# First batch set tile by tile, batch 1's loads one group earlier on GpSimd, eight empty steps ahead of the fourth piece of z

## Chip, cores and metric

One core of a Trainium2 chip runs the whole program. The metric is the time of one execution on the device in microseconds (us); lower is better. A profiled execution also has a span, from its first to its last instruction, and every time of a stretch or an instruction below is read from that one.

## What is computed

Eight batches of packed attention, then two feed-forward layers over all 4608 tokens:

```
p_packed = sm_attn(p, k, v)                  # 32 packed queries a head, 8 heads, 576 keys of 64
out      = sm_attn(q, p_packed, p_packed)    # 576 queries against the 32 packed rows
x  = out.transpose(0, 2, 1, 3).reshape(4608, 512)
h  = x @ moe_w_in ; x  = (h - tanh(h)) @ moe_w_out            # 512 -> 2048 -> 512
h  = x @ moe2_w_in; g  = s * relu(h)**2 + b ; out = g @ moe2_w_out
```

All weights arrive as 64-bit floats, and the kernel converts them to 32-bit floats itself, bit by bit. Products are made as three passes of 32-bit reduced floats: a matrix is split into a high and a low part, and high x low, high x high and low x high are summed.

## The kernel before

**Two stages.** Until about 800 us the kernel does attention and the first layer, batch by batch, and on the side turns the second layer's weights into a form kept in device memory. After that the class `SecondMLP` does the second layer. The change touches only the first stage.

**Tiles.** A batch has two halves of 288 tokens (hf 0 and 1), and a half has 16 tiles j of 128 hidden columns. Attention's last product is folded into the first layer: for each batch, `make_z` forms z (the packed values times `w_in`) in four pieces c of 512 columns, each used by four tiles, and `second_stage` forms the attention weights a of a half. For each tile, `mm1` (L464) multiplies z by a in six passes, an activation step forms h - tanh(h) and splits it into gh and gl, and `mm2` (L504), two tiles later in batch 0 and three later after that, multiplies by `w_out` in twelve passes.

**Three ways for the activation step.** "v" is `act1` and `split_g`: ScalarE makes tanh, VectorE subtracts (L473), ScalarE makes gh, VectorE makes gl (L135). "b" and "p" are `act_bank`: in "b" VectorE subtracts tanh in the bank of h (L481); in "p" TensorE subtracts it, with a 32-bit product by the matrix `minus` (L484). In both, ScalarE makes gh, TensorE subtracts gh from the bank (L487), and ScalarE copies the rest as gl. `HOW` gives the way of each tile of batch 0; later batches use "v" throughout.

**Batch 0 in four parts.** Its 32 tiles run as four parts of eight: tiles 0 to 7 of half 0, then of half 1, then tiles 8 to 15 of half 0, then of half 1. Meanwhile the first layer's weights are converted: `w1_steps(c, i)` is half a piece of `w_in`, `wo1_steps(j)` is 128 rows of `w_out`. One such conversion is a step on ScalarE (L119) and four on VectorE (L121, L123, L126, L129); a `wo1_steps` then splits, with ScalarE for the high part (L138) and VectorE or GpSimd for the low part (L140).

**Who sets the order.** Nothing is planned by cost. Each of these jobs is a generator, and each `yield` ends one step. `first_weights` runs groups of conversions, of z and of half 1's attention weights through `in_turn`, which goes round the members of a group and lets the next group make one step early. `attention` runs `first_weights`, then, for each batch b, z pieces 2 and 3 of b, half 1's weights of b, and `step_p`, two times `stage1`, z pieces 0 and 1 and half 0's weights of b+1. A `wait(n)` in it is n empty steps. The tile loop calls `slot()` six times a tile (once in mm1, once after the activation step, four times in mm2), and each call makes steps of `attention` (`fill`) and, on every third, of the second layer's conversion (`more`). In batch 0 until `w_out` is converted, part n makes `AFTER[n]` steps at once behind mm1 and spreads `SLOTS[n]` over six slots; after that each tile makes `CATCH_UP` steps at once and one in each slot. `until(key, fill)` makes steps at once until a thing that the next product needs has been issued.

**Queues.** SP issues most loads. GpSimd's queue issues batch 1's and later batches' k, v and q (`load_k`, `load_v`, `load_q`: L170, L177, L178, L240) and, in the kernel before, also runs ten of the low-part subtractions. Each engine works its queue in order.

Of the kernel before, what the change touches and what calls it, by code (L numbers as in the profile page):

```python
# [13 lines left out]
ALU = mybir.AluOpType  # L14
# [4 lines left out]
def pack_attention_two_mlps(ctx, tc, q, k, v, p, w_in1, w_out1, w_in2, w_out2, s_in, b_in, out):  # L19
# [33 lines left out]
    LAND = 14  # L53
    W_K, W_P, W_PK, W_PV, W_E, W_Q = 5, 1, 5, 1, 7, 5

    AFTER, SLOTS = (6, 5, 4, 1), (5, 3, 4, 1)
    HOW = "p" * 8, "b" * 8, "v" * 8, "v" * 8
    AHEAD, CATCH_UP, FIRST_W = 13, 4, (23, 24, 25, 26, 27, 40, 41, 42, 43, 44)
    EXP_LO, EXP_HI = 2.0 ** -15, 2.0 ** 16 * 1.875
    assert 2 * R == P and NB == 2 * C and 4 * M == P and 2 * D == P and H * D == DM  # L60

# [89 lines left out]
    def split_wo(j, tag, eng, x):  # L151
        t = wopool.tile([P, 2, DM], F32R, tag=f"wo{j}", name=f"{tag}_{j}")
        wo[j] = (t[:, 0], t[:, 1])
        yield from split_seq(t[:, 0], t[:, 1], x, eng)
# [294 lines left out]
    def wait(n):  # L449
        for _ in range(n):  # L450
            yield
# [80 lines left out]
    def both(gens):  # L532
        gens = list(gens)
        while gens:
            for g in list(gens):
                try:
                    next(g)
                except StopIteration:
                    gens.remove(g)
                    continue  # L540
                yield
# [14 lines left out]
    with tc.manual_schedule():  # L556
# [51 lines left out]
        def wo1_steps(j):  # L608
            while j == NF - 1 and ("wo", 13) not in done:
                yield  # L610
            src = stg["wo", j]
            x = words(src)[0].bitcast(F32)
            yield from to_f32(x, src, wopool.tile([P, 2, DM], I32, tag=f"wo{j}", name=f"t_{j}")[:, 0])
            yield from split_wo(j, "wo1", nc.gpsimd if 1 < j < 12 else nc.vector, x)
            done.add(("wo", j))
            if j in (5, 7):
                load_wo1(j + 3, j + 4)
            if j == 11:
                load_wo1(13)
            if j == NF - 1:  # L620
                free()
# [16 lines left out]

        def in_turn(*groups):

            groups = [[call_late(g) for g in group] for group in groups]
            for n, group in enumerate(groups):
                for i, _ in enumerate(both(group)):
                    yield
                    if i == min(AHEAD, 4 * len(group)) and n + 1 < len(groups):
                        for g in groups[n + 1]:
                            next(g)

        def call_late(f):
            g, *a = f  # L650
            yield from g(*a)

        def until(key, gen):
            forced.append(key)
# [16 lines left out]
        take_turn()  # L671
        load_wo1(0, 1, 2, 3, 4, 5, 6, 7)
        make_identity(nc, ident)
        nc.scalar.mul(minus, ident, -1.0)
        nc.vector.memset(ones, 1.0)

        run(step_p(0))
# [13 lines left out]
        def first_weights():  # L691
            yield from in_turn(
                [(w1_steps, 1, 0)], [(w1_steps, 1, 1)],
                [(wo1_steps, 0), (wo1_steps, 1)],
                [(first_z, 1), (wo1_steps, 2), (wo1_steps, 3)],
                [(wo1_steps, 4), (wo1_steps, 5)],
                [(second_stage, 0, 1), (wo1_steps, 6), (wo1_steps, 7)],
                [(w1_steps, 2, 0)], [(w1_steps, 2, 1)],
                [(wo1_steps, 8), (wo1_steps, 9)],
                [(first_z, 2), (wo1_steps, 10), (wo1_steps, 11)],  # L700
                [(w1_steps, 3, 0)], [(w1_steps, 3, 1)],
                [(wo1_steps, 12), (wo1_steps, 13), (second_loads,)],
                [(first_z, 3), (wo1_steps, 14), (wo1_steps, 15)])

        pend = []

# [66 lines left out]
        def make_zs(b, c):  # L773
            while (b - 1, 1, c) not in mm1_done:
                yield
            yield from make_z(b, c)
            done.add(("z", b, c))

        def attention():

            yield from first_weights()
            for b in range(B):
                if b:
                    for c in range(2, NCH):
                        yield from make_zs(b, c)
                    yield from second_stage(b, 1)
                if b + 1 == B:
                    return
                if b:
                    load_q(b + 1, 0)  # L790
                if b + 2 < B:
                    load_p(b + 2)
                nxt = (b + 2, 0) if b + 2 < B else None
                yield from step_p(b + 1)
                yield from stage1(b + 1, 0, (b + 1, 1), (b + 1, 1))
                yield from stage1(b + 1, 1, nxt, nxt)
                if b:
                    for c in range(2):
                        yield from make_zs(b + 1, c)
                    yield from second_stage(b + 1, 0)  # L800
                else:
                    yield from both([seq(make_zs(1, 0), make_zs(1, 1)), second_stage(1, 0)])
                load_q(b + 1, 1)
# [4 lines left out]
        def slot():  # L808
            ticks[0] += 1
            if owed[0]:  # L810
                owed[0] -= 1
                next(fill, None)
            if ("wo", NF - 1) not in done:
                n = SLOTS[part[0]]
                for _ in range(ticks[0] * n // 6 - (ticks[0] - 1) * n // 6):
                    next(fill)
                return
            if ticks[0] % 3 == 1:
                next(more, None)
            next(fill, None)  # L820

        owed = [0]

        def owe():
# [4 lines left out]
        for b in range(B):  # L829
            if b:  # L830
                parts = [(hf, range(NF)) for hf in range(2)]
            else:
                parts = [(hf, js) for js in (range(NF // 2), range(NF // 2, NF)) for hf in range(2)]
            for hf, js in parts:
                part[0] += 1
                last = (b == B - 1 and hf == 1)
                if last:
                    until(("a", b, hf), fill)
                    run(fill)
                    run(more)  # L840
                    att.close()
                    second = SecondMLP(tc, ctx, wslot, w2_d, wo2_d, x2t, g2_d, s_sb, bias, out)
                    fill = second.early(lambda c: (B - 1, 1, c) in mm1_done)
                acc = new_acc(f"{b}_{hf}_{js[0]}")
                for j in js:
                    c = j // CH
                    until(("z", b, c), fill)
                    until(("a", b, hf), fill)
                    h = mm1(b, hf, j, slot)
                    if ("wo", NF - 1) not in done:  # L850
                        for _ in range(AFTER[part[0]]):
                            next(fill)
                    elif ("a", 1, 0) not in done:
                        for _ in range(CATCH_UP):
                            next(fill)
                    if j % CH == CH - 1:
                        mm1_done.add((b, hf, c))
                    how = HOW[part[0]][j - js[0]] if b == 0 else "v"
                    on_pe = how != "v"
                    t = act_bank(h, f"{b}_{hf}_{j}", how == "p") if on_pe else act1(h, f"{b}_{hf}_{j}")  # L860
                    if on_pe:
                        next(t)
                    between = None
                    if pend and len(pend[-1]) == 5:
                        a_, j_, js_, t_, st_ = pend.pop()
                        if hasattr(t_, "send"):
                            def between(t_=t_, at=(a_, j_, js_), st_=st_):
                                pend.append((*at, next(t_), st_, True))
                        else:
                            pend.append((a_, j_, js_, split_g(t_, f"1_{b}_{hf}_{j}", nc.vector), st_, True))  # L870
                    slot()
                    if len(pend) + (between is not None) >= LAG[b > 0]:
                        a_, j_, js_, g_, st_, _ = pend.pop(0)
                        until(("wo", j_), fill)
                        mm2(a_, j_, js_, g_, owe if st_ and b else slot, between)
                        if st_:
                            store_x2(*st_, a_)
                            if b == 0 and st_[0] == 0 and js[0]:
                                load_part(0, hf)
                    elif between:  # L880
                        between()
                    if on_pe:
                        next(t)
                    pend.append((acc, j, js, t, (b, hf) if j == js[-1] else None))
# [451 lines left out]
```

## Time and profile before

| | us |
|---|---|
| median of 3 runs | 1511.85 (1509.85 to 1512.5) |
| profiled execution, its own time | 1508.74 |
| its span | 1507.0 |
| batch 0: part 0, from its first mm1 | 36.06 to 74.87 |
| part 1 | 74.87 to 111.54 |
| part 2 | 111.54 to 138.54 |
| part 3 | 138.54 to 171.25 |

A part begins where the first mm1 of its first tile begins. The span holds 1460.0 us of matmul records on TensorE (97%), 1070.7 on VectorE (71%), 753.1 on ScalarE (50%) and 333.0 on GpSimd (22%). Matmuls overlap and their ends are modelled, so a full TensorE row does not mean that it ran at its peak; what a stretch is worth is seen from the starts of its products and from the waits between them.

### The profile page before, as it was taken

How to read it: one execution, taken by the hardware profiler on the slowest of the kernel's cores; microseconds unless marked ns; L12 is line 12 of the kernel's file. 1: busy time of each engine (PE TensorE's matmuls, PEld its weight loads, DVE VectorE, ACT ScalarE, POOL GpSimd, SP SyncE). 2: the span in 40 equal slices, each digit the busy share in tenths (PEclk: the TensorE clock that was granted, in tenths of full speed). 3: DMA queues.
4: the chain of work that ended last, by engine and by line, in shares of the span. 5: the costliest groups of instructions: out<-in, count | busy, mean ns of one | idle time of the engine just before them, and what ended most of it. 6: DMA issues, size and time to landing. Idle time of an engine off the chain costs nothing. (4 is left out here: it accounts for less than half of the span.)

```text
span 1507.0 us, 28083 instructions
## 1 busy us (share of the span) xinstructions
PE 1460.0 (97%) x10512; PEld 1376.0 (91%) x10512; DVE 1070.7 (71%) x2074; ACT 753.1 (50%) x1459; POOL 333.0 (22%) x542
## 2 busy tenths in 40 slices
PE   6779899999999999999999999999999999999998
PEld 4668798998989899898999999999999999999998
DVE  4886878879787787876555767767777766565554
ACT  4554344444444444443344656656666655454443
POOL 0249452643446353523001000000021000000000
PEclk6899999999999999999999999999999999999999
DMA  9446455544535344433328456465487987676683
GB/s 275 168 138 166 109 143 136 153 140 121 153 102 150 104 130 117 119 79 129 114 100 309 188 226 257 171 238 224 186 312 279 309 267 191 216 243 197 219 246 84
DMA packets 252185, 271.62 MB, mean 180 GB/s; under 512 B 112784, under 2 KB 191888, under 8 KB 252048
## 3 DMA queue, kind: packets, MB, share of 16 engines
q1 hardware_dynamic: 225952, 222.68, 45.2%
q0 software_dynamic: 22368, 46.17, 11.5%
q8 instruction: 82, 1.34, 0.4%
q10 hardware_dynamic: 3728, 0.98, 0.3%
q14 instruction: 55, 0.45, 0.1%
HBM read 161.61 MB, written 108.13 MB: 179 GB/s over the span
## 5 line engine op out<-in xcount | busy, mean ns | idle before, releaser
L504 PE MATMUL acc<-gh,wo 128*128 128x288 f32 x2040 | 418.5, 296 | 0.2 <-DVE wo L140 0.2
L504 PEld LDWEIGHTS acc<-gh,wo 128*128 128x128 f32 x2040 | 329.8, 189 | 0.5 <-DVE wo L140 0.4
L504 PE MATMUL acc<-gl,wo 128*128 128x288 f32 x1020 | 309.8, 304 | 5.7 <-ACT wo L138 2.8
L472 ACT ACTIVATE t<-h 128x288 f32<-128x288 f32 x240 | 98.5, 411 | 297.9 <-PE h L464 261.9
L504 PEld LDWEIGHTS acc<-gl,wo 128*128 128x128 f32 x1020 | 192.3, 189 | 34.4 <-issue 20.0
L464 PE MATMUL h<-a2h,z 128*128 128x288 f32 x1024 | 214.0, 297 | 1.5 <-ACT z L445 1.5
L473 DVE TENSOR_TENSOR t<-h,t 128x288 f32<-128x288 f32 x240 | 107.7, 449 | 140.5 <-ACT t L472 139.3
L942 DVE TENSOR_TENSOR x<-B,x 128x768 fp32r<-128x768 f32 x158 | 147.2, 950 | 73.7 <-ACT x L1199 59.6
L240 POOL DMA_DIRECT2D q<-in_q_dram x224 | 135.2, 611 | 227.6 <-DVE qT L374 184.0
L464 PEld LDWEIGHTS h<-a2h,z 128*128 128x128 f32 x1024 | 165.0, 189 | 2.2 <-ACT z L445 1.7
L464 PE MATMUL h<-a2l,z 128*128 128x288 f32 x512 | 157.6, 308 | 8.3 <-ACT gl L488 6.3
L1043 PE MATMUL Y<-x,w 128*128 128x384 f32 x864 | 158.5, 336 | 0.0
L1269 PE MATMUL Y<-x,w 128*128 128x384 f32 x864 | 153.4, 335 | 0.2 <-DVE u L942 0.2
L170 POOL DMA_DIRECT2D k<-in_k_dram x224 | 136.4, 616 | 69.2 <-DVE kT L290 60.8
L1043 PEld LDWEIGHTS Y<-x,w 128*128 128x128 f32 x864 | 151.3, 188 | 0.0
L1269 PEld LDWEIGHTS Y<-x,w 128*128 128x128 f32 x864 | 150.2, 188 | 0.8 <-ACT x L1199 0.5
L464 PEld LDWEIGHTS h<-a2l,z 128*128 128x128 f32 x512 | 97.2, 190 | 25.3 <-ACT gl L488 9.3
L1199 ACT CAST x<-B 128x768 fp32r<-128x768 f32 x116 | 93.7, 833 | 40.7 <-DMA B<-g 26.4
L1043 PE MATMUL X<-x,w 128*128 128x384 f32 x576 | 108.0, 336 | 0.0
L1043 PE MATMUL Z<-x,w 128*128 128x384 f32 x576 | 107.9, 336 | 0.0
L135 DVE TENSOR_TENSOR gl<-t,gh 128x288 fp32r<-128x288 f32 x239 | 106.8, 447 | 0.0
L1269 PE MATMUL X<-x,w 128*128 128x384 f32 x576 | 103.0, 336 | 1.3 <-DVE w L942 1.3
(181 smaller groups left out, 2208.7 us busy)
## 6 DMA issues: line engine op xcount, KB each, us to landing
g<-g SPq DMA_DIRECT2D x190, 384.0 KB, 3.1
B<-g SPq DMA_DIRECT2D x116, 384.0 KB, 4.5
w<-w_d POOLq DMA_DIRECT2D x28, 512.0 KB, 6.5
B<-x2t SPq DMA_DIRECT2D x24, 384.0 KB, 5.3
g<-s SPq DMA_DIRECT2D x23, 384.0 KB, 2.7
out_dram<-g SPq DMA_DIRECT2D x184, 48.0 KB, 1.8
x2t<-xs SPq DMA_DIRECT2D x15, 576.0 KB, 3.6
w1s<-in_moe_w_in_dram SPq DMA_DIRECT2D x16, 512.0 KB, 8.0
```

What stands on the lines that cost most here:

```text
L135: (eng or nc.vector).tensor_tensor(out=lo, in0=x, in1=hi.bitcast(F32), op=ALU.subtract)
L170: nc.gpsimd.dma_start(out=t[p0:p0 + 32, e], in_=rows[a][:, e, :, u * 32:u * 32 + 32])
L240: nc.gpsimd.dma_start(out=t[p0:p0 + 32], in_=src.rearrange("(n r) d -> r n d", r=32))
L464: nc.tensor.matmul(h[:, :HB], zt[:, zi, g, f0:f0 + P], a[:, g], start=(n == 0), stop=(n == 3 * G - 1))
L472: nc.scalar.activation(t, h[:, :HB], AF.Tanh)
L473: nc.vector.tensor_tensor(out=t, in0=h[:, :HB], in1=t, op=ALU.subtract)
L504: nc.tensor.matmul(acc[m][:, :HB], w[:, m * P:(m + 1) * P], x, start=(j == js[0] and i == 0), stop=(j == js[-1] and i == 2))
L942: self.nc.vector.tensor_tensor(out=o, in0=a, in1=b, op=op)
L1043: self.nc.tensor.matmul(bank[:, f, :self.TH], w[:, f, a, kt], x[:, b, kt], start=(p in ("P1", "P5", "P6") and m == 0), stop=(m == 5), skip ...
L1199: self.nc.scalar.copy(self.xs[(7 * self.NBK + n) % self.XS][:, 0], self.ready[0])
L1269: nc.tensor.matmul(bank[:, ft, :T], w[:, kk, u, ft], x[:, v, kk], start=first and p in ("P1", "P5", "P6"), stop=last, skip_group_check=True)
```

## The change

- Batch 0's steps are set tile by tile: `STEPS` has a number for each of its 32 tiles, spread over that tile's slots; the steps made at once (`AFTER`, `CATCH_UP`) are gone. `HOW` is set tile by tile too: 17 "p", 13 "b" and 2 "v" where there were 8, 8 and 16. `FIRST` holds the same four parts in the same order.
- The low parts of rows 2 to 10 of `w_out` are subtracted by VectorE; GpSimd keeps row 11 alone.
- `in_turn` starts the next group earlier (behind two or three steps of a group instead of up to thirteen), and only its conversions.
- `second_loads` (batch 1's p by SP, and 34 loads of k, v and q by GpSimd) moves from the group of rows 12 and 13 to the group of the first half of `w_in`'s piece 3; z piece 3 goes with rows 12 and 13.
- `minus` is made by VectorE's memset and a GpSimd subtraction instead of ScalarE. The steps of attention behind which the first piece of `w_in` is converted (`FIRST_W`) are others.
- In every later batch eight empty steps come ahead of z piece 3.

```diff
-    AFTER, SLOTS = (6, 5, 4, 1), (5, 3, 4, 1)
-    HOW = "p" * 8, "b" * 8, "v" * 8, "v" * 8
-    AHEAD, CATCH_UP, FIRST_W = 13, 4, (23, 24, 25, 26, 27, 40, 41, 42, 43, 44)
+    STEPS = 8, 13, 14, 11, 14, 10, 12, 15, 0, 6, 9, 13, 9, 5, 0, 3, 5, 5, 11, 9, 6, 12, 8, 11, 18, 14, 15, 13, 12, 13, 10, 7
+    HOW = "ppbbpppppppvvbbppbppppbbbbbpbbbp"
+    FIRST = (0, 0, 8), (1, 0, 8), (0, 8, 16), (1, 8, 16)
+    FIRST_W = 11, 16, 18, 26, 28, 29, 31, 40, 43, 44
...
-            yield from split_wo(j, "wo1", nc.gpsimd if 1 < j < 12 else nc.vector, x)
+            yield from split_wo(j, "wo1", nc.gpsimd if j == 11 else nc.vector, x)
...
-            groups = [[call_late(g) for g in group] for group in groups]
+            groups = [[(f, f(*a)) for f, *a in group] for group in groups]
             for n, group in enumerate(groups):
-                for i, _ in enumerate(both(group)):
+                for i, _ in enumerate(both([g for _, g in group])):
                     yield
-                    if i == min(AHEAD, 4 * len(group)) and n + 1 < len(groups):
-                        for g in groups[n + 1]:
-                            next(g)
+                    if i == len(group) and n + 1 < len(groups):
+                        for f, g in groups[n + 1]:
+                            if f in (w1_steps, wo1_steps):
+                                next(g)
...
-        nc.scalar.mul(minus, ident, -1.0)
+        nc.vector.memset(csum, 0.0)
+        nc.gpsimd.tensor_tensor(out=minus, in0=csum[:, 0], in1=ident, op=ALU.subtract)
...
-                [(w1_steps, 3, 0)], [(w1_steps, 3, 1)],
-                [(wo1_steps, 12), (wo1_steps, 13), (second_loads,)],
-                [(first_z, 3), (wo1_steps, 14), (wo1_steps, 15)])
+                [(w1_steps, 3, 0), (second_loads,)], [(w1_steps, 3, 1)],
+                [(first_z, 3), (wo1_steps, 12), (wo1_steps, 13)],
+                [(wo1_steps, 14), (wo1_steps, 15)])
...
                     for c in range(2, NCH):
+                        yield from wait(8 * (c == 3))
                         yield from make_zs(b, c)
...
-            if ("wo", NF - 1) not in done:
-                n = SLOTS[part[0]]
-                for _ in range(ticks[0] * n // 6 - (ticks[0] - 1) * n // 6):
+            if ("wo", NF - 1) in done and ticks[0] % 3 == 1:
+                next(more, None)
+            if ("a", 1, 0) in done or tile[0] >= len(STEPS):
+                next(fill, None)
+                return
+            n = STEPS[tile[0]]
+            for _ in range(ticks[0] * n // 6 - (ticks[0] - 1) * n // 6):
+                if ("a", 1, 0) not in done:
                     next(fill)
-                return
-            if ticks[0] % 3 == 1:
-                next(more, None)
-            next(fill, None)
...
                     h = mm1(b, hf, j, slot)
-                    if ("wo", NF - 1) not in done:
-                        for _ in range(AFTER[part[0]]):
-                            next(fill)
-                    elif ("a", 1, 0) not in done:
-                        for _ in range(CATCH_UP):
-                            next(fill)
...
-                    how = HOW[part[0]][j - js[0]] if b == 0 else "v"
+                    how = HOW[tile[0]] if b == 0 else "v"
```

## Rows read from the trace of the kernel before

**Rows 1.** The page's 40 slices: TensorE's busy share in tenths

```profile
PE   6779899999999999999999999999999999999998
```

**Rows 2.** Busy time by stretch, one for each part of batch 0

```profile
36.06:74.87 38.81, 30.39 (x178) 24.02 (x178) 34.19 (x60) 23.35 (x49) 8.16 (x6) 0.88 0.48 177
74.87:111.54 36.67, 27.25 (x186) 21.81 (x186) 32.63 (x53) 20.98 (x47) 16.12 (x20) 0.95 0.47 143
111.54:138.54 27.00, 25.28 (x228) 22.05 (x228) 18.27 (x46) 13.36 (x38) 23.61 (x40) 1.00 0.75 178
138.54:171.25 32.71, 29.25 (x273) 21.96 (x271) 24.52 (x65) 13.46 (x37) 18.85 (x32) 1.00 0.48 120
```

**Rows 3.** TensorE's waits from 36 to 190: us, times, longest

```profile
PE h L464 <- ACT gl L488: 6.3, 8, 2.0
PE acc L504 <- ACT wo L138: 2.8, 1, 2.8
PE zp L367 <- DVE z L435: 2.7, 2, 2.5
```

**Rows 4.** VectorE in order of time: start, us, line

```profile
36.93 0.69 DVE L121 TENSOR_SCALAR w<-w 128x1024 f32<-128x1024 f32 x1 [0.55 <-DMA wo1s<-in_moe_w_out_dram]
...
40.79 0.69 DVE L121 TENSOR_SCALAR w<-w 128x1024 f32<-128x1024 f32 x1
...
44.64 0.76 DVE L121 TENSOR_SCALAR t<-t 128x512 f32<-128x512 f32 x2
...
48.60 1.30 DVE L140 TENSOR_TENSOR wo<-wo1s,wo 128x512 fp32r<-128x512 f32 x2
49.82 0.75 DVE L121 TENSOR_SCALAR t<-t 128x512 f32<-128x512 f32 x2
...
55.75 0.99 DVE L121 TENSOR_SCALAR t<-t 128x512 f32<-128x512 f32 x2 [2.10 <-ACT t L119]
...
90.42 1.28 DVE L121 TENSOR_SCALAR t<-t 128x512 f32<-128x512 f32 x2
```

**Rows 5.** GpSimd in order of time

```profile
56.92 2.76 POOL L140 TENSOR_TENSOR wo<-wo1s,wo 128x512 fp32r<-128x512 f32 x2 [55.61 <-ACT wo L138]
...
99.05 6.78 POOL L170 DMA_DIRECT2D k<-in_k_dram  x10
```

**Rows 6.** Instructions by line and shape, 0 to 230

```profile
L473 DVE TENSOR_TENSOR t<-h,t 128x288 f32<-128x288 f32 x37 | 16.6, 449 | 22.5 <-ACT t L472 22.4
```

**Rows 7.** TensorE in order of time, two places

```profile
66.79 0.65 PE L484 MATMUL h<-t,minus 128*128 128x288 f32 x2
...
67.41 0.43 PE L464 MATMUL h<-a2h,z 128*128 128x288 f32 x2
...
184.28 0.29 PE L464 MATMUL h<-a2l,z 128*128 128x288 f32 x1
...
186.68 0.29 PE L464 MATMUL h<-a2l,z 128*128 128x288 f32 x1
```

**Rows 8.** ScalarE in order of time, in the preamble

```profile
15.03 1.15 ACT L119 ACTIVATE w<-w1s 128x1024 f32<-128x1024 f32 x1
```

**Rows 9.** TensorE's z products (L367): batch 1's last, later batches

```profile
169.63 1.69 PE L367 MATMUL zp<-w,pblk 64*32 64x512 f32 x16 [2.48 <-DVE z L435]
...
226.95 1.23 PE L367 MATMUL zp<-w,pblk 64*32 64x512 f32 x16
235.89 1.09 PE L367 MATMUL zp<-w,pblk 64*32 64x512 f32 x16
...
343.50 1.09 PE L367 MATMUL zp<-w,pblk 64*32 64x512 f32 x16
348.76 1.04 PE L367 MATMUL zp<-w,pblk 64*32 64x512 f32 x2 [0.78 <-DVE z L435]
350.36 1.09 PE L367 MATMUL zp<-w,pblk 64*32 64x512 f32 x14 [0.56 <-DVE z L435]
...
712.55 1.37 PE L367 MATMUL zp<-w,pblk 64*32 64x512 f32 x16
```

More of the change, by code (lines that the diff above doesn't have):

```diff
@@ L639, in in_turn @@
         def in_turn(*groups):
-            groups = [[call_late(g) for g in group] for group in groups]
+            groups = [[(f, f(*a)) for f, *a in group] for group in groups]
             for n, group in enumerate(groups):
-                for i, _ in enumerate(both(group)):
+                for i, _ in enumerate(both([g for _, g in group])):
                     yield
-                    if i == min(AHEAD, 4 * len(group)) and n + 1 < len(groups):
-                        for g in groups[n + 1]:
-                            next(g)
-        def call_late(f):
-            g, *a = f
-            yield from g(*a)
+                    if i == len(group) and n + 1 < len(groups):
+                        for f, g in groups[n + 1]:
+                            if f in (w1_steps, wo1_steps):
+                                next(g)
         def until(key, gen):
@@ L812, in slot @@
                 next(fill, None)
-            if ("wo", NF - 1) not in done:
-                n = SLOTS[part[0]]
-                for _ in range(ticks[0] * n // 6 - (ticks[0] - 1) * n // 6):
+            if ("wo", NF - 1) in done and ticks[0] % 3 == 1:
[6 more added lines that the diff above has]
+                if ("a", 1, 0) not in done:
                     next(fill)
-                return
-            if ticks[0] % 3 == 1:
-                next(more, None)
-            next(fill, None)
+        tile = [-1]
         owed = [0]
@@ L832, in pack_attention_two_mlps @@
             else:
-                parts = [(hf, js) for js in (range(NF // 2), range(NF // 2, NF)) for hf in range(2)]
+                parts = [(hf, range(j0, j1)) for hf, j0, j1 in FIRST]
             for hf, js in parts:
@@ L846, in pack_attention_two_mlps @@
                     c = j // CH
+                    tile[0] += 1
                     until(("z", b, c), fill)
```

## Prediction

> **What bounds the kernel now.** I read the page's slices first, then stretches cut at the first mm1 of each part of batch 0, then TensorE's waits, then the engines' queues in order of time. TensorE is full from the fourth slice of 37.7 us on [rows 1], so only the stretch before it and short stalls behind it can give anything. Cut by parts [rows 2], parts 0 and 1 belong to VectorE: it is busy 34.19 of 38.81 us and 32.63 of 36.67, while TensorE has 30.39 and 27.25 with latencies counted in. In parts 2 and 3 it is the other way round, TensorE 25.28 of 27.00 and 29.25 of 32.71, VectorE 18.27 and 24.52. A tile alone needs 2.40 us of TensorE, as two neighbours starting at 184.28 and 186.68 show [rows 7], eight need 19.2. So the four parts, 135 us for 77 us of tiles, are uneven: conversion is crowded into the first two while VectorE idles a third of the third. The waits say the same: TensorE waits most for ScalarE's gl [rows 3], whose inputs stand in the queues behind conversion made at once.
>
> **Steps tile by tile.** I counted yields. `first_weights` is some 180 steps in the new form, `step_p` 3, two `stage1` 82, z pieces 0 and 1 with half 0's weights of batch 1 46: 311, and STEPS sums to 311. By part it is 97, 45, 67, 102. Before, it was about 80, 64, 66 and 80 and the rest by `until` at once. So the same jobs are done, but part 1 loses about 20 steps and ends with the first half of `w_in`'s piece 3, where the kernel before had gone on to its second half and rows 12 and 13 of `w_out`. These move into part 2.
>
> What a job costs VectorE [rows 4]: half a piece of `w_in` goes from 36.93 to 40.79, 3.86 us; two `wo1_steps` from 44.64 to 48.60, 3.96; two low parts from 48.60 to 49.82, 1.22. A subtraction of a tile is 0.45 [rows 6]; "v" has two, "b" one, "p" none. On TensorE the 32-bit product of a "p" delays the next product from 66.79 to 67.41 [rows 7], 0.62 less the 0.13 of a pass (2.40/18): 0.49; the gh product of "p" and "b" is one more pass, 0.13. So "p" costs 0.62, "b" 0.13.
>
> **Low parts from GpSimd to VectorE.** Nine of 0.61 are 5.5 us more VectorE work. Against that, VectorE is slowed while GpSimd subtracts: at 55.75 and 90.42 the same pair of L121 that takes 0.75 at 49.82 takes 0.99 and 1.28, with GpSimd in the queue beside it [rows 4, 5]. The seven such rows from 55.75 to 90.42 hold 5.0 us too much, 4.5 in part 0. I take these as recovered; the bounds are nothing recovered and all.
> The Trainium skill (SBUF — State Buffer, "Who interferes with whom") has it that the two engines share a port pair, and that VectorE in a two-port mode, or with two inputs in SBUF against a GpSimd operation that reads SBUF, blocks fully. These rows agree in kind; by it each of nine subtractions of 1.38 could hold VectorE, 12.4 us freed instead of 5.0, and the sum would be 7 lower.
>
> **Part 0.** VectorE: +3.7 for six low parts, +0.9 for two tiles turned from "p" to "b", -4.5 for GpSimd. That is nothing. Of the 4.6 us in which VectorE idles, 2.1 are one wait for ScalarE's first conversion step at 55.75 [rows 4], which the new `in_turn` issues earlier. I take -0.9; bounds -3 and +3.5 (nothing recovered, the idle stays).
>
> **Part 1.** VectorE loses half a piece of `w_in` (3.86) and rows 12 and 13 with their low parts (5.18), gains three low parts (1.8), loses 0.5 of slowing; its tiles go from eight "b" (3.6) to two "v", two "b" (2.7), -0.9. 36.67 - 8.6 = 28.0. TensorE's need: 19.2, plus 4 x 0.62 + 2 x 0.13, plus z piece 2 (1.09 [rows 9] and some 0.5): 23.5. With VectorE still ahead I take 28.0, **-8.7**. Bounds: 24 (neither waits for the other, -12.7) and 31.8 (TensorE works at the 74% of its old part 1, -4.9).
>
> **Parts 2 and 3.** VectorE's 9.0 us land in part 2, whose 18.3 of 27 leave 8.7 free; there the sixteen "v" that would cost it 14.4 become seven "p", nine "b" at 4.1. So VectorE has room, at TensorE's expense: 7 x 0.62 + 9 x 0.13 = 5.5. Z piece 3's product, just ahead of part 2 before, falls into it, +1.1. Batch 1's last z stalls 2.48 and runs 0.6 over the 1.09 of an undisturbed one [rows 9]; with eight steps ahead of it this goes, -3.1. Both parts, with the two z that move into batch 1: **+3.5**. Bounds: -2 if the remaining short waits go as well, +8 if the weights now made just ahead of use stop TensorE (the second rival).
>
> **Batch 1's loads.** 34 loads of 0.68 (ten from 99.05 [rows 5]) are 23 us of GpSimd's queue. Before, they stood behind the last pair of subtractions; now they come a group earlier, some 5 us, with only row 11's low part ahead. Behind them queue `stage1`'s next k and v loads, which come later anyway. p goes past nothing on SP that waits for it. What an earlier landing gives is first used a part later: nothing, and if the cover went, one transpose of k would wait.
>
> **Preamble.** `FIRST_W` puts a ScalarE step of 1.15 [rows 8] ahead of the first exponentials. It can wait for its load; the value product behind waits for v. `minus` is first used in z piece 0's correction, long after. Nothing, bounds +1 and -1, about one such step.
>
> **Eight empty steps.** From batch 2 on, z piece 3 follows piece 2 before VectorE has freed the banks. In batch 3 it starts after 0.78 idle and ends at 351.45 instead of 349.85, in all 2.4 us; the six of batches 2 to 7, the last at 712.55 (1.37 long), lose 6.1 [rows 9]. TensorE is the bound there, so this is time. Eight slots are 8/6 of a tile, over 3.2 us, and would cover each. I take three quarters, **-4.5**; bounds -6.1 and 0. The cost is nothing as long as attention has slots to spare: 192 a batch, 177 steps, 185 now.
>
> **Sum.** -0.9 - 8.7 + 3.5 - 4.5 = -10.6 against the profiled execution's 1508.74, giving 1498.1. The median of the runs is 3.1 above that execution, so **1501** as a median.
>
> **Rivals.**
> *The work comes back as waits (about 1508).* Conversions now end close to use: z piece 3 is done some three steps ahead of tile 20, rows 14 and 15 some two tiles ahead. Before, one such meeting, `mm2` waiting for a row's high part, cost 2.8 [rows 3]. Two or three of these in part 2 take 6 to 8 of the gain. For it: each queue is served in order and part 2 is tight on both engines. Against: that wait stands once in all of batch 0 before.
> *The empty steps come late (about 1520, slower).* The place is the first tile of batches 2 to 7. Z piece 1 of the next batch can't be issued before mm1 of tile 7 of half 1; if eight slots push it beyond that, half 0's weights end at the next batch's first tile and `until` issues the rest at once. Then six batches pay the eight slots, 3.2 us each, 19.2 on top of my sum. It decides at the spare steps: batch 2's pieces 0 and 1 lie 226.95 to 235.89 apart, 8.9 us [rows 9], where pieces 2 and 3 lie 5.3 apart (343.50 to 348.76) with 0.8 of stall, so about 4.5 are spare, against 3.2 for bare tiles and somewhat more with attention's products between. It fits, narrowly.
> *Nothing recovered on VectorE (about 1510).* If VectorE's slowing was not GpSimd's doing, parts 0 and 1 get 5 us longer than I say, and with part 1 at the slow end (another 4) 1.6 of the 10.6 are left. Against: the slowed rows lie where GpSimd is busy.
> *GpSimd's loads starve (about 1524).* If busy VectorE held back the issue of these loads as they come deeper into the conversion stretch, batch 1's attention would be late. At 99.05 the issue takes 0.68 each in the middle of such work [rows 5]; three times that would add 46 us to the queue and half of it to the end.
> The Trainium skill (SBUF — State Buffer, "SBUF: two separate sides") warns of that: descriptors for GpSimd's DMAs can't be written while VectorE is in a two-port mode, with 620 ns growing to some 3100. The trace does not bear it out: 0.68 a load, while VectorE ran L121 and L123.
> *More than the forecast (about 1492).* Parts 1 to 3 lose their short waits too, 4 in part 1 (its lower bound) and 3 behind it, and the later batches all 6.1.
>
> **Chances and range.** Forecast 0.60 (own range 1495 to 1506), more 0.10, waits come back 0.15, nothing recovered 0.06, late 0.07, starved 0.02. Less than 0.2% of the time, 3 us, can't be told from no change. Half of "waits come back" counts as faster: faster 0.60 + 0.10 + 0.07 = 0.77; same 0.08 + 0.06, and 0.01 of the late, 0.15; slower 0.08. The range of 1491 to 1511 leaves out the late, the starved and a little at the bottom.
>
> **What would show it.** Right: part 1 shrinks to about 28 us and part 2 stays near 29; no VectorE row of L121 or L123 is stretched; the stall ahead of z piece 3 is gone in every batch; the time from 800 us on is moved whole. Wrong: TensorE waiting in part 2 for `wo` or z; batches 2 to 7 starting with a wait for a2l; GpSimd's loads above 1 us; part 0 longer than 39.

## The result, and the profile after

| | before | after |
|---|---|---|
| median of 4 runs, us | 1510.85 (1508.24 to 1512.5) | 1494.97 (1494.37 to 1496.64) |
| profiled execution, its own time | 1508.74 | 1496.64 |
| its span | 1507.0 | 1494.9 |

The ratio is 0.9903, with a 95% interval of 0.9886 to 0.992: about 1% faster. By medians the gain is 15.9 us, but the profiled executions differ by only 12.1: that of before was low among its runs, that of after was the highest of its four. Everything below is read from these two and adds up to 12.1. Lines of the batch code are one higher than before (mm1 L465, mm2 L505, the z product L368, low parts L141, conversion L122 to L130).

The page of the changed kernel: its span, and TensorE's busy share in 40 slices, to set against [rows 1].

```profile
span 1494.9 us, 28130 instructions
...
PE   6899999999999999999999999999999999999998
```

TensorE is full from the third slice instead of the fourth, so the gain lies early. The changed kernel's busy time by part of batch 0, with the columns of [rows 2] (span of the part, then PE, PEld, DVE, ACT, POOL busy, granted clock, DMA share, GB/s):

```profile
36.17:75.04 38.87, 31.48 (x174) 25.54 (x174) 35.96 (x71) 24.77 (x50) 0.00 (x0) 0.81 0.53 200
75.04:99.37 24.33, 24.19 (x178) 21.87 (x176) 23.10 (x39) 17.02 (x38) 7.06 (x9) 1.00 0.39 133
99.37:125.63 26.26, 26.17 (x206) 23.60 (x204) 18.95 (x36) 17.77 (x48) 21.08 (x35) 1.00 0.71 171
125.63:158.22 32.59, 31.13 (x326) 24.53 (x324) 21.55 (x59) 15.79 (x45) 27.01 (x45) 1.00 0.58 138
```

Part 1 gives the whole gain: 36.67 to 24.33, -12.3. Parts 0, 2 and 3 are within 0.8 of what they were. In part 1 VectorE's busy time fell from 32.63 to 23.10, its idle time from 4.0 to 1.2, TensorE's idle time from 9.4 to 0.1, and the granted clock rose from 0.95 to 1.00. Batch 1 therefore starts at 158.22 instead of 171.25, 13.0 earlier.

What held up part 1 of the kernel before stands in ScalarE's waits there (74.87 to 111.54), the longest in total:

```profile
ACT gh L485 <- DVE h L481: 12.0, 5, 2.8
```

At five "b" tiles ScalarE waited for VectorE's subtraction, which stood behind conversion in VectorE's queue. TensorE in turn waited 3.6 for gh and 2.7 for gl, and VectorE 3.1 for ScalarE's tanh. In part 1 of the changed kernel the wait for the subtraction is gone, and the view lists no wait of TensorE at all. TensorE's waits from 36 to 190, against [rows 3]:

```profile
PE acc L505 <- ACT wo L139: 2.8, 1, 2.8
PE h L465 <- ACT gl L489: 1.8, 2, 1.3
PE h L465 <- DVE a2l L419: 1.4, 1, 1.4
PE zp L368 <- DVE w L130: 1.3, 1, 1.3
```

The wait for gl shrank from 6.3 to 1.8; the one for the high part of a row of `w_out` stayed (it is at 50 us, in part 0). The wait for a2l stood before too (2.0 in three stops, the longest 1.4); the one of z for converted weights grew from 0.3 to 1.3, in part 0.

Later batches: z products in order of time in the changed kernel, against [rows 9].

```profile
165.86 1.09 PE L368 MATMUL zp<-w,pblk 64*32 64x512 f32 x16
...
308.14 1.61 PE L368 MATMUL zp<-w,pblk 64*32 64x512 f32 x16
318.27 1.09 PE L368 MATMUL zp<-w,pblk 64*32 64x512 f32 x16
...
336.77 1.09 PE L368 MATMUL zp<-w,pblk 64*32 64x512 f32 x16
343.58 1.09 PE L368 MATMUL zp<-w,pblk 64*32 64x512 f32 x16
```

The pair at 336.77 and 343.58 is pieces 2 and 3 of batch 3, and the stall between them is gone, as in all later batches. But piece 0 of the same batch, made earlier at 308.14, now runs 1.61 and not 1.14: it waits for VectorE's copy of the packed values (by the waits of the weight loads 2.6 us in five batches, 0.4 in one before). And the z at 165.86 stands within batch 1, where before it stood ahead of it at 169.63: 1.1 us that only changed sides.

To see what later batches gained, take the store that follows the last product of batch 1's second half and of batch 7's first, in SyncE's queue. Before:

```profile
270.64 0.56 SPq L522 DMA_DIRECT2D x2t<-xs  x1
...
762.73 0.52 SPq L522 DMA_DIRECT2D x2t<-xs  x1
```

After:

```profile
261.24 0.56 SPq L523 DMA_DIRECT2D x2t<-xs  x1
...
751.65 0.52 SPq L523 DMA_DIRECT2D x2t<-xs  x1
```

Between the two stores lie 492.1 us before and 490.4 after: 1.7 gained in batches 2 to 7. From its first product to the first store, batch 1 takes 99.4 before and 103.0 after, 3.6 more, of which 1.1 is the z that moved in. The second stage starts 11.1 earlier and is 1.0 shorter (709.6 for 710.6). Over the traces of all kernels here it takes 709.3 to 711.3 with the same code, so the 1.0 is not shown to come from the change.

### The profile page after: what moved, and what is told of

Read it like the earlier page. It is cut to its first block, busy times and chain, and to the rows that moved or that the text cites. A ratio compares the mean times of both kernels' runs of the same rounds, so it can differ in the third digit from the quotient of the medians.

```text
span 1494.9 us, 28130 instructions
## 1 busy us (share of the span) xinstructions
PE 1464.0 (98%) x10544; PEld 1383.1 (93%) x10544; DVE 1060.7 (71%) x2061; ACT 759.5 (51%) x1472; POOL 321.6 (22%) x534
## 4 chain that ended last, share of the span: by engine, by line
PE 87%; DVE 5%; DMA 3%; ACT 2%; SPq 1%; issue 1%; POOL 1%; DVEq 0%; ACTq 0%
PE acc L505 25%; PE h L465 12%; PE Y L1040 10%; PE Y L1266 10%; PE X L1040 7%; PE Z L1040 7%; PE Z L1266 6%; PE X L1266 6%; PE zp L368 2%; SPq L195 1%; POOL k L171 1%; PE s L368 1%; PE pv L340 1%; PE s L271 1%; DMA B<-g 1%
## 5 line engine op out<-in xcount | busy, mean ns | idle before, releaser
L505 PE MATMUL acc<-gh,wo 128*128 128x288 f32 x2040 | 419.9, 297 | 0.2 <-DVE wo L141 0.2
L505 PEld LDWEIGHTS acc<-gh,wo 128*128 128x128 f32 x2040 | 330.5, 189 | 0.5 <-DVE wo L141 0.4
L505 PE MATMUL acc<-gl,wo 128*128 128x288 f32 x1020 | 310.7, 305 | 3.4 <-ACT wo L139 2.8
L473 ACT ACTIVATE t<-h 128x288 f32<-128x288 f32 x226 | 92.9, 411 | 257.2 <-PE h L465 219.9
L505 PEld LDWEIGHTS acc<-gl,wo 128*128 128x128 f32 x1020 | 192.6, 189 | 31.9 <-issue 19.8
L465 PE MATMUL h<-a2h,z 128*128 128x288 f32 x1024 | 214.1, 297 | 0.1
L474 DVE TENSOR_TENSOR t<-h,t 128x288 f32<-128x288 f32 x226 | 101.3, 448 | 136.2 <-ACT t L473 135.0
L465 PEld LDWEIGHTS h<-a2h,z 128*128 128x128 f32 x1024 | 165.4, 190 | 1.4 <-ACT z L446 0.5
L465 PE MATMUL h<-a2l,z 128*128 128x288 f32 x512 | 158.7, 310 | 4.1 <-ACT gl L489 1.8
L465 PEld LDWEIGHTS h<-a2l,z 128*128 128x128 f32 x512 | 97.5, 190 | 19.4 <-issue 6.8
L1040 PE MATMUL Z<-x,w 128*128 128x384 f32 x576 | 107.9, 336 | 0.0
L1266 PE MATMUL Z<-x,w 128*128 128x384 f32 x576 | 102.2, 335 | 0.0
```

The source lines that it names most:

```text
L465: nc.tensor.matmul(h[:, :HB], zt[:, zi, g, f0:f0 + P], a[:, g], start=(n == 0), stop=(n == 3 * G - 1))
L473: nc.scalar.activation(t, h[:, :HB], AF.Tanh)
L474: nc.vector.tensor_tensor(out=t, in0=h[:, :HB], in1=t, op=ALU.subtract)
L505: nc.tensor.matmul(acc[m][:, :HB], w[:, m * P:(m + 1) * P], x, start=(j == js[0] and i == 0), stop=(j == js[-1] and i == 2))
L1040: self.nc.tensor.matmul(bank[:, f, :self.TH], w[:, f, a, kt], x[:, b, kt], start=(p in ("P1", "P5", "P6") and m == 0), stop=(m == 5), skip ...
L1266: nc.tensor.matmul(bank[:, ft, :T], w[:, kk, u, ft], x[:, v, kk], start=first and p in ("P1", "P5", "P6"), stop=last, skip_group_check=True)
```

## The experiments

**Theory:** the gain is made by taking conversion out of part 1, where VectorE was full, and the other edits are worth little each. **Rivals:** it is not which part has the steps but that they come one at a time instead of in bursts; or that VectorE runs free of GpSimd; or that the empty steps give most of it.

All kernels compute everything. Each ran beside the kernel before on the same chip. "To changed" is the difference of the medians, with the first row's 1496.04 for the changed kernel; between kernels on different chips the ratios are the better measure.

| run | median us | ratio to before, 95% | to changed |
|---|---|---|---|
| changed kernel again | 1496.04 | 0.9899 (0.9883 to 0.9914) | |
| 1 same steps, crowded as before | 1511.60 | 1.0013 (1.0004 to 1.0022) | +15.6 |
| 2 steps at once, as before | 1513.74 | 1.0019 (1.0010 to 1.0028) | +17.7 |
| 3 only `STEPS`, on the kernel before | 1513.65 | 1.0021 (1.0009 to 1.0032) | +17.6 |
| 4 low parts on GpSimd | 1500.71 | 0.9933 (0.9920 to 0.9945) | +4.7 |
| 5 old ways of the tiles | 1501.84 | 0.9942 (0.9929 to 0.9955) | +5.8 |
| 6 next group begun late | 1508.21 | 0.9987 (0.9977 to 0.9997) | +12.2 |
| 7 no empty steps | 1498.18 | 0.9916 (0.9902 to 0.9929) | +2.1 |
| 8 only empty steps, on the kernel before | 1508.87 | 0.9990 (0.9981 to 0.9999) | +12.8 |
| 9 empty steps from batch 2 on | 1494.45 | 0.9902 (0.9888 to 0.9915) | -1.6 |
| 10 empty steps split | 1500.66 | 0.9937 (0.9924 to 0.9949) | +4.6 |
| 11 loads a group later | 1496.22 | 0.9910 (0.9896 to 0.9924) | +0.2 |

**The changed kernel again**, as a base.

> The changed kernel itself, beside the others of this call: 0.990 of the kernel before, as measured; its parts of batch 0 near 38.9, 24.3, 26.3 and 32.6 us.

The medians of the two sets agree within 1.1 us. Its first two parts by busy time:

```profile
35.51:73.33 37.82, 30.21 (x173) 24.44 (x173) 34.57 (x69) 23.74 (x50) 0.00 (x0) 0.83 0.52 196
73.33:99.08 25.75, 24.43 (x179) 21.97 (x177) 24.49 (x41) 17.93 (x39) 7.06 (x9) 1.00 0.42 144
```

One kernel's part 0 and part 1 thus move by 1.0 and 1.4 us between executions; together they took 63.2 and 63.6. The split of the result's trace is the odd one: in runs 7, 9 and 10, with the same code up to there, part 0 takes 37.5 to 38.0 and part 1 25.7 to 25.8. By these part 0 is about 1.0 shorter than in the kernel before and part 1 about 10.9.

**1 and 2: the steps back in part 1.** Run 1 spreads 96, 64, 48 and 104 steps evenly over the four parts: part 1 has the 64 of the kernel before, not 45. Run 2 takes the whole old rule, with its steps at once.

```diff
-    STEPS = 8, 13, 14, 11, ...
+    STEPS = (12,) * 8 + (8,) * 8 + (6,) * 8 + (13,) * 8
```

```diff
-            n = STEPS[tile[0]]
+            n = SLOTS[part[0]]
...
                     h = mm1(b, hf, j, slot)
+                        for _ in range(AFTER[part[0]]):
+                            next(fill)
```

> The changed kernel with as many steps in each part as before about (96, 64, 48, 104), spread evenly, none made at once. If part 1 got short because 19 steps (9 us of VectorE) left it: part 1 about 8 us longer, part 2 shorter by 1 at most, so about 7 us slower than the changed kernel. If it got short because steps are no longer made at once behind mm1: within 2 us of the changed kernel.

> The changed kernel with the pace of the kernel before (steps at once behind mm1, and slots by part). Theory one (work moved out of part 1): as the evenly crowded one, about 7 us slower than the changed kernel. Theory two (steps at once hold back ScalarE's and VectorE's part of a tile): 3 us or more slower than the evenly crowded one, in all 8 to 12.

Both lose the whole gain. Run 1 makes no step at once, so it is not the lack of bursts that the gain hangs on. Run 2 is 2.1 us slower still, and only one of its eleven times lies under run 1's median; but its numbers in the other parts differ too, so this is no price of bursts. Run 1's busy time, part 1 first, then three stretches of it:

```profile
73.78:114.18 40.40, 30.29 (x193) 24.69 (x193) 31.91 (x52) 20.61 (x44) 14.96 (x22) 0.87 0.40 125
...
82.00:86.00 4.00, 0.00 (x0) 0.00 (x0) 4.00 (x10) 1.02 (x3) 0.00 (x0) 0.99 0.00 0
86.00:90.00 4.00, 4.00 (x25) 2.06 (x26) 2.91 (x7) 1.49 (x5) 0.00 (x0) 0.58 0.41 147
...
107.00:113.00 6.00, 5.88 (x25) 4.22 (x26) 3.90 (x9) 1.40 (x3) 5.22 (x9) 0.50 0.29 61
```

Part 1 takes 40.40, 14.7 more than in the changed kernel, and this is more than VectorE's added work of 7.4 (31.91 for 24.49). The same run's ScalarE, VectorE and TensorE in order of time say why:

```profile
84.26 1.29 DVE L130 SCALAR_TENSOR_TENSOR wo1s<-wo1s,t 128x512 int32<-128x512 int32 x2
84.97 0.67 ACT L139 CAST wo<-wo1s 128x512 fp32r<-128x512 f32 x1 [5.16 <-DVE wo1s L130]
85.54 0.71 ACT L99 COPY xs<-acc 128x288 f32<-128x288 f32 x2
86.00 0.61 PE L505 MATMUL acc<-gl,wo 128*128 128x288 f32 x1 [5.08 <-ACT xs L99]
...
102.82 1.06 PE L368 MATMUL zp<-w,pblk 64*32 64x512 f32 x8 [1.79 <-DVE w L130]
107.12 1.93 PE L368 MATMUL zp<-w,pblk 64*32 64x512 f32 x8 [3.24 <-DVE w L130]
```

ScalarE's cast of a row's high part was issued early and stands 5.16 us in its queue until VectorE has converted the row. Behind it stands the copy that empties the accumulator, and TensorE waits 5.08 for that copy. Later z piece 2 waits 1.79 and 3.24 for its two halves of converted weights, with all tile products behind it. After each such stop TensorE's granted clock falls: 0.58 from 86 to 90, 0.50 (the lower level, 1.2 GHz) from 107 to 113, while the same products run on. Of the 14.7 us, 8.8 are more idle time of TensorE (10.1 for 1.3) and 5.9 more busy time. A mean clock of 0.87 over 40.40 us is, as an estimate, 10.5 us at the lower level (0.13 doubled, times 40.40), which at the upper would have been 5.3: most of the 5.9. Outside part 1 the differences nearly cancel: part 2 is 1.1 shorter, part 3 4.1 longer, and batch 1 up to its store about 5 shorter.

Run 1 does not tell number and placing apart. It has 64 steps in part 1 for 45, and it spreads them evenly, where `STEPS` has none on that part's first and seventh tile. No run has the 45 spread evenly.

**3: the new numbers alone, on the kernel before.**

```diff
-    AFTER, SLOTS = (6, 5, 4, 1), (5, 3, 4, 1)
+    STEPS = 8, 13, 14, 11, ...
...
-                n = SLOTS[part[0]]
+            n = STEPS[tile[0]]
```

> The kernel before with the steps tile by tile alone (old ways of the tiles, low parts on GpSimd, old groups and no empty steps). If the pace is what makes part 1 short: part 1 about 27 to 29 us instead of 36.7 and 6 to 9 us faster than before. If the pace only pays with the ways of the tiles and VectorE's low parts, which cost 5.8 and 4.7 when taken out one at a time: within 3 us of before.

Slower than the kernel before by 3.5, though part 1 did get shorter. Its busy time:

```profile
74.61:106.27 31.66, 26.13 (x170) 22.35 (x171) 23.52 (x40) 18.56 (x42) 11.23 (x13) 0.89 0.44 142
```

VectorE's work in part 1 fell by 9.1 (32.63 to 23.52) and the part by 5.0. But part 0 grew by 1.5, part 2 by 4.9 (31.85) and part 3 by 3.1 (35.76). The theory in its plain form falls: the numbers take time out of part 1 by themselves, but without the order of jobs around them all of it comes back in the other parts. One place in part 2, TensorE in order of time:

```profile
124.58 0.40 PE L464 MATMUL h<-a2h,z 128*128 128x288 f32 x1 [3.67 <-ACT z L445]
```

(Its lines are those of the kernel before.) Its groups are the old ones, in which z piece 3 comes later than the numbers are set for, and the first tile that needs it waits 3.67.

**4: low parts of rows 2 to 10 back on GpSimd.**

```diff
-split_wo(j, "wo1", nc.gpsimd if j == 11 else nc.vector, x)
+split_wo(j, "wo1", nc.gpsimd if 1 < j < 12 else nc.vector, x)
```

> The changed kernel with the low parts of rows 2 to 10 on GpSimd again. The prediction's term: VectorE's slowing (5 us) and the work taken off it (5.5) cancel, so within 1 us. Rival one, nothing was recovered: about 4 us faster with them on GpSimd. Rival two, GpSimd's operations hold VectorE for their whole length: 5 us or more slower.

The kernel is 4.7 slower. Parts 0 and 1 together take 67.8 in its trace, where the changed kernel has 63.2 and 63.6. Its part 0 by busy time:

```profile
34.65:75.64 40.99, 31.01 (x173) 25.43 (x174) 37.90 (x65) 24.09 (x50) 8.70 (x6) 0.81 0.51 188
```

VectorE and GpSimd in order of time:

```profile
54.53 1.88 DVE L122 TENSOR_SCALAR t<-t 128x512 f32<-128x512 f32 x2
54.75 2.82 POOL L141 TENSOR_TENSOR wo<-wo1s,wo 128x512 fp32r<-128x512 f32 x2 [52.90 <-ACT wo L139]
56.33 1.86 DVE L124 TENSOR_SCALAR t<-t 128x512 int32<-128x512 int32 x2
...
60.78 3.11 POOL L141 TENSOR_TENSOR wo<-wo1s,wo 128x512 fp32r<-128x512 f32 x2 [3.21 <-ACT wo L139]
61.59 2.59 DVE L124 TENSOR_SCALAR t<-t 128x512 int32<-128x512 int32 x2
...
67.59 2.98 DVE L395 TENSOR_TENSOR t<-t,st 128x288 f32<-128x288 f32 x2
```

The first three of VectorE's pairs take 0.75 each in the changed kernel and the last 0.90 (two of 0.45). All four lie beside a subtraction of GpSimd (its third starts at 67.49), and no other row of VectorE in this part is stretched by over 0.1: 6.2 us of slowing for 8.7 of GpSimd's subtractions.

**5: the ways of the tiles as before**, "v" in parts 2 and 3.

```diff
-    HOW = "ppbbpppppppvvbbppbppppbbbbbpbbbp"
+    HOW = "p" * 8 + "b" * 8 + "v" * 16
```

> The changed kernel with the ways of the kernel before: eight p, eight b, sixteen v. The prediction's theory: parts 2 and 3 are TensorE's, the p and b cost it 5.5 us there, VectorE has room; so 4 to 5 us faster than the changed kernel in parts 2 and 3, against up to 1 us lost in part 1 (eight b on VectorE). The rival: with conversion moved into part 2 VectorE sets it, and sixteen v put 10 us back on VectorE: 4 us or more slower.

Slower by 5.8: part 1 28.00 and part 2 29.65, where the changed kernel again has 25.75 and 26.25; part 3 is 0.4 shorter. Part 2 by busy time:

```profile
101.36:131.01 29.65, 25.64 (x186) 21.51 (x187) 24.87 (x50) 15.25 (x40) 19.98 (x33) 1.00 0.54 129
```

Neither engine is full (TensorE 25.64, VectorE 24.87 of 29.65), and TensorE's products, 186 for 205, took 0.5 less than in the changed kernel. TensorE's waits in part 2, where the changed kernel again has none:

```profile
PE zp L368 <- DVE w L130: 1.4, 1, 1.4
PE acc L505 <- DVE gl L136: 1.1, 1, 1.1
PE h L465 <- ACT z L446: 0.9, 1, 0.9
```

A "v" tile crosses VectorE's queue twice, and VectorE has 5.9 us more work in this part than in the changed kernel again (24.87 for 18.96). TensorE waits there for weights that VectorE converts, for VectorE's gl and for ScalarE's z. VectorE's own largest wait from 73 to 163 is for the tanh of "v" tiles:

```profile
DVE t L474 <- ACT t L473: 7.1, 8, 1.4
```

That wait does not explain the difference: in part 2 it is 2.6 in three stops, and the changed kernel again waits 2.8 in three stops there for the tanh of "b" tiles.

**6: the next group begun late, and z too, as before.**

```diff
-                    if i == len(group) and n + 1 < len(groups):
+                    if i == min(13, 4 * len(group)) and n + 1 < len(groups):
                         for f, g in groups[n + 1]:
-                            if f in (w1_steps, wo1_steps):
-                                next(g)
+                            next(g)
```

> The changed kernel with the next group started as late as before (behind step 8 of 14, or the last of five), z among them. The prediction's term: ScalarE's first step is late again, VectorE waits 2.1 us once, 1 us slower in part 0. The rival, that in a VectorE-bound part each late first step is lost: 3 us or more slower, in parts 0 and 1.

Slower by 12.2, spread over all parts: 40.92, 27.66, 28.42, 36.35. VectorE's waits in part 0:

```profile
DVE wo L141 <- ACT wo L139: 2.7, 3, 1.2
DVE w L122 <- ACT w L120: 2.3, 2, 1.8
```

(The changed kernel again has 0.4 of the second there and none of the first.) And TensorE in part 3, in order of time:

```profile
161.00 0.40 PE L465 MATMUL h<-a2l,z 128*128 128x288 f32 x1 [2.25 <-ACT gl L489]
```

Two things are mixed here: conversion's first ScalarE step comes later, and z's first step is made early, which shifts the count of steps against `STEPS` by some five. They were not tried apart.

**7 to 10: the empty steps.** Run 7 leaves them out:

```diff
-                        yield from wait(8 * (c == 3))
```

Run 8 adds that same line to the kernel before, and nothing else. Run 9 has them only from batch 2 on:

```diff
-                        yield from wait(8 * (c == 3))
+                        yield from wait(8 * (c == 3 and b > 1))
```

Run 10 puts five ahead of z piece 3 and three ahead of the next batch's z piece 0:

```diff
-                        yield from wait(8 * (c == 3))
+                        yield from wait(5 * (c == 3))
...
                     for c in range(2):
+                        yield from wait(3 * (c == 0))
                         yield from make_zs(b + 1, c)
```

> The changed kernel without the eight empty steps. The prediction's term: TensorE is the bound there, so the stalls ahead of z piece 3 are time, and the kernel gets 4.5 us slower than the changed one. The rival, from the two traces: z piece 0 of the next batch is then held back by its own condition again and loses the stall that it has in the changed kernel (1.6 to 2.0 us long instead of 1.1 in five batches), so only 0 to 2 us are lost.

> The kernel before with the eight empty steps alone. The prediction's term: 4.5 us faster than before, plus up to 3 for batch 1's last z (2.48 idle). The rival: 0 to 2 us faster, as the stall turns up again at the next batch's z piece 0 behind its DVE copy of pblk.

> The changed kernel with the eight empty steps from batch 2 on, none in batch 1. Between the changed kernel and the one without empty steps, batches 2 to 7 take 451.2 and 455.5 us, but batch 1 is the shorter in the one without, by some 1.5 us when the eight slots by which its end is marked later are taken off. If that is batch 1's lateness, this is 1 to 2 us faster than the changed kernel. If it is not, within 1 us, or slower by batch 1's share of the stalls.

> The changed kernel with five empty steps ahead of z piece 3 and three ahead of the next batch's z piece 0. If the stall ahead of piece 3 went on to piece 0 because that now follows the DVE copy of pblk at once, three steps there give back 0.5 to 0.9 us in five batches: 2 to 4 us faster than the changed kernel. If the stall is no time of the whole, within 1 us.

The same two stores in run 7:

```profile
259.63 0.56 SPq L523 DMA_DIRECT2D x2t<-xs  x1
...
753.21 0.52 SPq L523 DMA_DIRECT2D x2t<-xs  x1
```

Batches 2 to 7 take 493.6 without the empty steps and 490.4 with them: 3.2 gained there. Batch 1 from its first product to the first of these stores takes 102.4 without, 103.0 with them, and 101.0 in run 9. Run 9 differs from the changed kernel only in the eight steps of batch 1, so these cost 2.0 there. The whole is 2.1 by medians, and each of run 7's four times lies above each of the changed kernel's four beside it.

In the kernel before, the same line brings 1.2 (run 8), and none of it in batches 2 to 7, which take 492.9 for 492.1. Part 3 gets 4.2 shorter and batch 1 2.5 longer; 1.1 of both is the z that changes sides. The kernel before and run 7 have the same code in batches 2 to 7 and take 492.1 and 493.6, so differences of 1.5 arise there without any edit to it.

Run 9 is the lowest median of all, but its interval lies on that of the changed kernel: no better version is shown. Run 10 was meant to mend the wait of z piece 0; that product stayed long (1.4 to 1.8 us in five batches), and the kernel lost 4.6, 4.2 of it in batches 2 to 7 (494.6 by the two stores). I did not find why.

**11: batch 1's loads a group later.**

```diff
-                [(w1_steps, 3, 0), (second_loads,)], [(w1_steps, 3, 1)],
-                [(first_z, 3), (wo1_steps, 12), (wo1_steps, 13)],
+                [(w1_steps, 3, 0)], [(w1_steps, 3, 1)],
+                [(first_z, 3), (wo1_steps, 12), (wo1_steps, 13), (second_loads,)],
```

> The changed kernel with batch 1's loads back in the group of rows 12 and 13. The prediction's term: nothing, within 1 us of the changed kernel. The rival: they land some 5 us later, the transposes of k in part 2 wait for them and hold the tiles there, 2 us or more slower.

No difference (+0.2). In its trace part 2 is 1.2 longer than in the changed kernel again (27.40) and part 3 1.9 shorter (30.97).

## Why the prediction was right

The prediction of 1501 (1491 to 1511) and "faster" came true. By its own steps the account of the profiled executions is:

| | predicted | measured |
|---|---|---|
| preamble | 0 | +0.1 |
| part 0 | -0.9 | +0.1 |
| part 1 | -8.7 | -12.3 |
| parts 2 and 3, with the z that moved | +3.5 | -0.9, and +1.1 for one z |
| eight empty steps | -4.5 | |
| batches 1 to 7, that z apart | 0 | +0.9, with the empty steps |
| second stage | 0 | -1.0 |
| sum | -10.6 | -12.1 |

Batches 1 to 7 took 1.95 more in all, of which 1.1 is that z. The median, 1494.97, lies just under the forecast's own range of 1495 to 1506, and 6 under the 1501.

*Part 1: right in mechanism, too small.* With the new numbers alone part 1 got 5.0 shorter (run 3); with 64 evenly spread steps back in it, 14.7 longer (run 1). The old ways of the tiles make 2.3 of it (run 5, 28.00). VectorE's busy time came out as reckoned (24.0 predicted, 23.1 and 24.5 measured). The term was mis-sized because I left VectorE's 4.0 us of idle time where it was, and it fell to 1.2. The range had this as the lower bound of 24 us and the rival "more than the forecast". In the kernel before that idle time was mostly VectorE's 3.1 us of waiting for tanh, while ScalarE waited 12.0 for VectorE's subtractions and TensorE 6.3 for its gh and gl: each engine stopped behind another's queue. Run 1 shows stops of the same kind, and TensorE at the lower clock after them.

*Parts 2 and 3: the price of the ways had the wrong sign.* I charged 5.5 us of TensorE time for "p" and "b" in place of "v". TensorE did get busier (part 2 25.28 to 26.17, part 3 29.25 to 31.13), but by 2.8 in all, half the charge, and its idle time went down by more (1.7 to 0.1 and 3.5 to 1.5), so the parts did not grow. Of that idle time 2.5 is the stall ahead of batch 1's last z, which the sum had counted; of the two z that it let move into batch 1, one did. Run 5 shows the sign: with "v" part 2 is 3.4 longer and part 3 0.4 shorter. The sum counted VectorE's free time and not when its results are due: in run 5 VectorE is busy 24.87 of 29.65 in part 2, and TensorE still waits 3.4 there for what VectorE and ScalarE make late.

*Low parts: taken as nothing, worth 4.7.* I set VectorE's 5.5 us of added work against 5.0 of recovered slowing. Run 4's slowing is 6.2 of 8.7 in part 0 alone, where the kernel before had 4.5 of 8.16. The Trainium skill (SBUF — State Buffer, "Who interferes with whom") speaks of a full block for such pairs; the new rows lie nearer to that than the rows that I went by, and the rival "nothing recovered" is out.

*Early start of the next group: taken as 0.9, at most 3; 12.2 in run 6.* Part 0, where I put the 0.9, did not shrink in the result's trace: VectorE has 1.8 us more work there (35.96 for 34.19) and idles 2.9 for 4.6. In the changed kernel again and in runs 7, 9 and 10 it is 0.8 to 1.4 shorter than before. What part of the 12.2 is the early ScalarE step and what the shift of the count is open.

*Empty steps: -4.5 predicted, 2.1.* The step that failed is that these stalls, TensorE being the bound there, are time of the whole. The stalls went, but z piece 0 now waits for its packed values, and the eight steps of batch 1 cost 2.0 there (run 9). Over batches 2 to 7 the gain is 3.2 against run 7, 1.7 against the kernel before, and nothing in the kernel before itself (run 8). The rival "empty steps late" did not come.

*Loads: nothing, as predicted.* GpSimd in order of time in the changed kernel:

```profile
93.98 7.26 POOL L171 DMA_DIRECT2D k<-in_k_dram  x10
```

That is 0.73 a load in the middle of conversion, for 0.68 before; the rival "loads starve" is out. "The work comes back as waits" is out too: the wait for `wo` in [rows 3] is there once, as before, and in part 2 TensorE has no wait in the view.

That the total came out near is in part luck, as errors offset each other. Parts 1 to 3 came out 6.9 better than forecast (3.6 in part 1, 3.3 in parts 2 and 3) and the second stage 1.0 better; the empty steps with batches 1 to 7 came out 5.4 worse (0.9 longer for 4.5 shorter) and part 0 1.0 worse. Nor do the single prices add: taken out one at a time the parts cost 2.1, 4.7, 5.8, 12.2 and 15.6, some 40 together, where the whole is worth 14 to 16. Each was measured with `STEPS` set for the others, and out of step with them the numbers are worse than the old rule (run 3).

## What to carry to other kernels

Cut the span by stage, and for each count the busy time of every engine and also its idle time: where both engines idle, look for queues that hold each other up. Moving work out of such a stage can give more than the work itself (part 1 here: 12.3 for 9.5 of VectorE's time), but only if it does not come back where it lands (run 3). When steps are spread over engines that work in order, look at what stands behind each early-issued instruction: one cast that waits for its input stops the copy behind it, and through that TensorE. A table of steps fits one order of jobs; change the two together, and don't price them apart.

## What the runs showed of the hardware

After 5 us in which TensorE was idle (81 to 86 in run 1), its granted clock was 0.58 over the next 4 us; after stops of 1.8 and 3.2 us close together, ending at 107, it was 0.50 for 6 us. The stops themselves are thus only part of their price: by the estimate above, about 5.3 us of the 14.7 came from the lower clock. And GpSimd's subtractions of 128x512 slowed VectorE, working beside them, by 6.2 us for 8.7 us of their own time (run 4, part 0).
